# P times V of a sliding-window attention in 64x32 array tiles, with both row halves stored and added later

## The chip, the cores and the metric

The kernel runs on one core of a Trainium2 chip. A core has a matrix engine (TensorE, PE in the profile, with its weight loads as PEld), a vector engine (VectorE, DVE), a scalar engine (ScalarE, ACT), a general engine (GpSimd, POOL), a synchronisation engine that mostly issues transfers (SyncE, SP), and 16 DMA engines. The metric is the device time of one execution in microseconds (us); the median of the runs counts.

## The reference

A layer computes attention and an MLP on the same 2048 tokens of 512 features and mixes them with a gate per token:

```
q, k, v = split(x @ wqkv)            # 32 heads of 16
s = q @ k.T * 16**-0.5               # masked to 0 <= i - j < 256
a = softmax(s) @ v @ wo
b = gelu(layernorm(x) @ w1 + b1) @ w2 + b2     # 512 -> 1792 -> 512
out = g * a + (1 - g) * b            # g = sigmoid(sum(x * gate_w))
```

All of it is fp32. Each query sees itself and the 255 tokens before it, so a block of 128 keys meets at most three blocks of 128 queries.

## The kernel before

Products of q, k, v and of the MLP are made in a faster fp32 format in three terms (high x high, low x high, high x low). P times V alone is in plain fp32, and each of its matmuls leaves two records in the trace.

The kernel has three stages. The first (to about 148 us) makes q, k and v, stores q and k to DRAM in a stacked layout, and normalises the tokens. The second (148 to 486 us) is attention and the first MLP layer, woven together. The third (486 us on) is the second MLP layer (`mlp2`, 56 items of 12 matmuls) with the output projection (`attn_out`) at four places.

In the second stage the heads come in 8 groups p of four. Four kinds of work are ordered by a string of letters, the order table, which `run` walks through one letter at a time, and TensorE executes in that order:

- **S** (`s_pair`): scores of two heads for one block of queries. DVE reduces each to its row maxima (L377), which go through DRAM back into the stacked q.
- **T** (`st_pair`): transposed scores of two heads for one block kb of keys, maxima taken off within the matmul. ACT takes the exponential (L418) into a tile `p` (or `xq`) of 128 keys x 4 heads x 384 queries, POOL sets what is out of the window to 0 (L420).
- **P** (`pv`, L427): P times V. The four heads of a group stand in four column tiles of 32 of the array and run side by side. One P makes the output of two query blocks (256 queries) from up to four key blocks, in matmuls of 128 keys by 256 or 128 queries. V has a column of ones for each head, so the sum of the exponentials comes along. ACT copies the 256 columns to half of a tile (L443), and each second P sends the tile to `osc` in DRAM.
- **f** (`fill`): one step of an MLP unit of the first layer: two matmuls on the two row halves of the array (L639).

PSUM is a ring of four bank pairs, `b0` to `b3`. An MLP unit keeps one for its 24 steps; S, T and P take turns on the other three. Pools: `work` has six `p` tiles and nine `t` tiles in the second stage, `xq` gives two more P tiles (kb 3, 7, 11, 15). Work that is due later is put on a list (`after(k, ...)`) that advances by one with each key block in the second stage and with each item in the third. SP issues nearly all transfers, in its own program order.

In the third stage `attn_out(c)` starts for 512 queries at the items in `AO`. For each of four groups of heads it loads the attention output and the reciprocal sums from DRAM into tiles `or`, multiplies them on POOL (L822), splits the product into a high part on ACT and a low part on DVE, and multiplies by wo (L840). `attn_sums` makes the reciprocals from 16 small loads ahead of that. DVE makes the high and low parts of the hidden tiles (L706, L139) that `mlp2` multiplies, in the same queue.

The start of the kernel (`first_units`, L268) converts weights and the first tokens on ACT and takes low parts on DVE.

## Time and profile before

| | |
|---|---|
| median of 3 runs | 685.75 us (685.74 to 688.0) |
| profiled execution | 687.4 us, span 685.7 us |
| PE busy | 677.5 us (99%) |
| DVE, ACT, POOL busy | 473.4, 362.8, 277.6 us |
| granted TensorE clock, mean | 0.996 |
| moved by DMA | 137.95 MB |

The span runs from the first to the last instruction; the time of an execution has some more around it. A row of a group gives the line of the kernel, the engine, the operation, output and inputs, the shape, the count; behind the bar the busy time and the mean of one in ns; behind the second bar the idle time of the engine ahead of these instructions and what ended it. A row of a timeline gives the start in us, the length, the engine and line, and how many alike were merged. Shapes of matmuls read as weights, then moving data: `128*32 128x256` is 128 rows by 32 columns of weights and 256 columns streamed. Durations of matmuls include the way through the array, and neighbours overlap.

### The profile page before, as it was taken

The numbers are of one execution on the slowest core, as the hardware profiler recorded it, in microseconds if no ns is written. First come the engines' busy times: TensorE is split into PE (matmuls) and PEld (weight loads), VectorE is DVE, ScalarE is ACT, GpSimd is POOL, SyncE is SP. The second block draws the span as 40 slices with busy tenths as digits, with TensorE's granted clock in tenths as the row PEclk, the third lists the DMA queues.
The fourth block names the chain that finished last, engine by engine and source line by source line (L and its number), as shares of the span: only waits on it lengthen the run. The fifth ranks groups of instructions, "written<-read, shape, count | busy, mean of one in ns | idle before, by whom it ended". The sixth has DMA issues, their size and how long they took to land.

```text
span 685.7 us, 16341 instructions
## 1 busy us (share of the span) xinstructions
PE 677.5 (99%) x5738; PEld 543.2 (79%) x5738; DVE 473.4 (69%) x1495; ACT 362.8 (53%) x580; POOL 277.6 (40%) x553
## 2 busy tenths in 40 slices
PE   8999999999999999999999999999999999999997
PEld 6877777876778888788878778777788888888886
DVE  5378866698877877767877878786587453736623
ACT  6332223357776776777667668768763022324210
POOL 8210019816465655656547547647411030210300
PEclk9999999999999999999999999999999999999999
DMA  8899877876666677675676655736994371832801
GB/s 270 274 311 297 287 239 263 259 224 215 186 219 210 193 213 232 202 215 159 208 234 217 187 186 165 206 119 189 315 281 149 125 202 50 241 115 92 235 1 61
DMA packets 91446, 137.95 MB, mean 201 GB/s; under 512 B 15108, under 2 KB 38852, under 8 KB 91236
## 3 DMA queue, kind: packets, MB, share of 16 engines
q1 hardware_dynamic: 90324, 135.20, 63.2%
q8 instruction: 45, 0.74, 0.5%
q0 software_dynamic: 320, 1.05, 0.4%
q10 hardware_dynamic: 720, 0.66, 0.3%
q14 instruction: 37, 0.30, 0.1%
HBM read 81.53 MB, written 54.28 MB: 198 GB/s over the span
## 4 chain that ended last, share of the span: by engine, by line
PE 93%; DMA 4%; DVE 2%; ACT 1%; SPq 0%; issue 0%; DVEq 0%; ACTq 0%
PE ps_b L639 23%; PE ps_a L872 22%; PE ps_b L435 12%; PE ps_d L311 10%; PE ps_b L416 7%; PE ps_o L840 6%; PE ps_b L372 6%; PE ps_d L346 4%; DMA t<-in_xa 2%; PE ps_d L296 1%; DMA qk<-t 1%; DMA t<-in_wqk 1%; PE ps_x L372 1%; DVE us L879 0%; DVE xq L139 0%; ACT x L142 0%
## 5 line engine op out<-in xcount | busy, mean ns | idle before, releaser
L377 DVE CUSTOM_DVE_ANT_0 scr<-ps_b,wide 128x384 bf16<-128x384 f32 (+1 forms) x472 | 227.6, 530 | 63.6 <-PE ps_b L372 61.7
L639 PE MATMUL ps_b<-x,w 64*128 64x512 f32 x1344 | 208.6, 392 | 0.7 <-DVE t L139 0.7
L420 POOL TENSOR_SCALAR_AFFINE_SELECT p<-p 128x256 f32<-128x256 f32 x368 | 140.1, 411 | 129.2 <-ACT p L418 127.9
L418 ACT ACTIVATE p<-ps_b 128x768 f32<-128x768 f32 x192 | 146.6, 795 | 30.8 <-PE ps_b L416 23.3
L872 PE MATMUL ps_a<-x,h 128*128 128x512 f32 x648 | 149.0, 389 | 0.0
L872 PEld LDWEIGHTS ps_a<-x,h 128*128 128x128 f32 x648 | 121.6, 188 | 25.3
L639 PEld LDWEIGHTS ps_b<-x,w 64*128 64x128 f32 x1344 | 128.4, 186 | 10.2 <-DVE t L139 1.1
L416 PE MATMUL ps_b<-q,k 50*128 50x384 f32 (+5 forms) x512 | 89.9, 345 | 0.2 <-DVE mx L377 0.2
L372 PE MATMUL ps_b<-k,q 62*128 62x384 f32 (+3 forms) x472 | 81.9, 336 | 0.0
L822 POOL TENSOR_TENSOR or<-or,or 128x512 f32<-128x512 f32 x16 | 23.1, 1446 | 138.8 <-DMA or<-rd 133.5
L142 ACT ACTIVATE t<-ps_b 128x256 f32<-128x256 f32 (+1 forms) x116 | 52.8, 487 | 43.5 <-PE ps_b L435 35.2
L435 PE MATMUL ps_b<-p,v 128*32 128x256 f32 (+1 forms) x1472 | 71.8, 330 | 0.0
L416 PEld LDWEIGHTS ps_b<-q,k 50*128 50x128 f32 (+1 forms) x512 | 49.3, 184 | 16.7 <-DVE mx L377 3.6
L435 PEld LDWEIGHTS ps_b<-p,v 128*32 128x32 f32 x1472 | 42.4, 110 | 23.1 <-issue 2.9
L372 PEld LDWEIGHTS ps_b<-k,q 62*128 62x128 f32 (+1 forms) x472 | 46.5, 185 | 10.1 <-ACT p L418 1.4
L420 POOL TENSOR_SCALAR_AFFINE_SELECT xq<-xq 128x256 f32<-128x256 f32 x112 | 44.0, 418 | 22.1 <-ACT xq L418 21.1
L418 ACT ACTIVATE xq<-ps_b 128x768 f32<-128x768 f32 (+1 forms) x64 | 44.2, 706 | 14.1 <-PE ps_b L416 11.4
L142 ACT ACTIVATE t<-ps_d 128x512 fp32r<-128x512 f32 x32 | 19.0, 596 | 54.3 <-PE ps_d L311 49.3
L142 ACT ACTIVATE a<-or 128x512 fp32r<-128x512 f32 x16 | 10.1, 633 | 67.3 <-POOL or L822 67.3
L840 PE MATMUL ps_o<-wo,a 128*128 128x512 f32 x192 | 45.5, 389 | 0.0
L139 DVE TENSOR_TENSOR h<-e,h 128x512 fp32r<-128x512 f32 x54 | 39.6, 733 | 4.6
L377 DVE DVE_READ_ACCUMULATOR2_ANT mx<- 128x1 f32 x512 | 42.4, 83 | 0.0
(94 smaller groups left out, 744.9 us busy)
## 6 DMA issues: line engine op xcount, KB each, us to landing
qk<-t SPq DMA_DIRECT2D x72, 256.0 KB
hp<-t SPq DMA_DIRECT2D x54, 256.0 KB
e<-hp SPq DMA_DIRECT2D x54, 256.0 KB
k<-qk SPq DMA_DIRECT2D x112, 98.0 KB
q<-qk SPq DMA_DIRECT2D x112, 98.0 KB
osc<-t SPq DMA_DIRECT2D x30, 256.0 KB
w<-w SPq DMA_DIRECT2D x28, 256.0 KB
qk<-qk SPq DMA_DIRECT2D x24, 256.0 KB
```

What stands on the lines that cost most here:

```text
L139: eng.tensor_tensor(out=lo, in0=src, in1=f32(hi), op=ALU.subtract)
L142: act.activation(dst, src, AF.Copy)
L311: pe.matmul(o, a[:, dt * 128:(dt + 1) * 128], b[:, dt * C:(dt + 1) * C], start=n == 0, stop=n == 11)
L372: pe.matmul(o[:, e, :n], qs[pr][r:k, qb * 128:qb * 128 + 128], ks[pr][r:k, t0:t0 + n], start=True, stop=True)
L377: dve.tensor_tensor_reduce(out=sc[:, :n], in0=o[:, e, :n], in1=wide[:, 384 - n:], scale=1.0, scalar=NEG, op0=ALU.add, op1=ALU.max, accum_o ...
L416: pe.matmul(o[:, e, :w], ks[pr][r:k, kb * 128:kb * 128 + 128], qs[pr][r:k, kb * 128:kb * 128 + w], start=True, stop=True)
L418: act.activation(pt[:, :, :w], o[:, :, :w], AF.Exp, scale=0.25)
L420: pool.affine_select(out=pt[:, :, a:a + 128], in_=pt[:, :, a:a + 128], pattern=[[0, 2], [sgn, 128]], base=b, channel_multiplier=-sgn, comp ...
L435: pe.matmul(a[32 * h:32 * h + 32, at:at + w], vs[:, kb, v:v + 32], pts[p, kb][:, h, fr:fr + w], start=n == 0, stop=n == len(parts) - 1, sk ...
L639: pe.matmul(o[:, e], w[kt // 4][r:r + 64, k, m:m + 128], y[r:r + 64, a:a + C], start=n == 0, stop=n == 23)
L840: pe.matmul(a, hl[g][x][:, b * 128:b * 128 + 128], wos[g][:, k], start=n == 0, stop=n == 11)
L872: pe.matmul(accs[c][b], x[:, b * 128:(b + 1) * 128], w, start=f == 0 and n == 0, stop=f == FT - 1 and n == 2)
```

## The change

P times V takes four query blocks (512 queries) at once, in array tiles of 64 rows by 32 columns: two halves of the keys of a block times four heads, eight tiles. The upper 64 keys of each block accumulate in one bank of a pair, the lower 64 in the other. Since each half block has its own window of queries, the pieces are 320 columns wide at most, cut at the edges of the 512, and the order of the key blocks differs between the halves so that pieces of one width meet. ACT copies both banks at once into a tile `o` of 128 x 2 x 512, and one transfer stores both halves to `osc`, which has twice the size. The sums are added in `attn_sums`, and the outputs in `attn_out` on DVE, ahead of POOL's product. The reciprocals have a tag of their own in the `xq` pool, `t` has seven tiles for nine, the first output projection starts at item 9 (7 before), and the order table is a new one with 31 letters P for 63 (a last P stands behind it). At the start, the first tile of x is converted by DVE, as an addition of zeros.

```diff
-ORDER = ("TSTfffSfTSffffTSffTfTfSfTffSffTSffTfSfTfSffSPTSSTPSTTPSTffSfTfSffTffTSffTffSfSPTfSfTffTffTSfffSffSPT"
...
+ORDER = ("TfTffSffTfSfTSfffTSfTffTfSfTfSffTfSfTSffTSffSSPSTfffSffSffTfffSTffSffTfSffTfTffffSSPSTTSTSTSTTST"
+         "STffSffTSfffSffSPSffTfffTSfTffTffTTSffTfffSSPSfTfffTfSfTffSffTTffSfTffSfTfSfffTSffTffSPSTffffTfSfTff"
...
+         "SffTffSfSPSTSTTSTSTffSffTSfffTfTffffTTPfTTfffTffffTffffTTPffTfTfffTfTfffTffTfTffTfTfPfTfffTfTTfff")
...
-AO = (7, 16, 28, 42)
+AO = (9, 16, 28, 42)
...
-    osc = dram.tile([8, 128, S], F32, name="osc")
+    osc = dram.tile([2, 8, 128, S], F32, name="osc")
...
             for t in range(2):
                 if dt % 2 == 0:
                     k = slice(dt * 128, dt * 128 + 256)
                     copy(ws[t][:, 0, k], raws[t][:, k])
+                    if not dt and not t:
+                        hi(0, lambda h, x: dve.tensor_tensor(out=h, in0=x, in1=f32(blank), op=ALU.add))
                     lo_part(ws[t][:, 1, k], raws[t][:, k], ws[t][:, 0, k])
-                if t == 0:
-                    hi(dt)
+                if t == (not dt):
+                    if dt:
+                        hi(dt)
                     lo(dt)
...
-    def pv(p, j, last):
+    def pv(p, j):
         flush()
-        a = two()[:, 0]
-        parts = ((-1, 0, 128, 256), (-2, 0, 256, 128), (0, 0, 0, 256), (1, 128, 0, 128))[0 if j else 2:]
-        for n, (d, at, fr, w) in enumerate(parts):
-            kb = 2 * j + d
-            for h in range(4):
-                v = (4 * p + h) * VW
-                pe.matmul(a[32 * h:32 * h + 32, at:at + w], vs[:, kb, v:v + 32], pts[p, kb][:, h, fr:fr + w],
-                          start=n == 0, stop=n == len(parts) - 1, skip_group_check=True, tile_position=(0, 32 * h))
...
+        a = two()
+        ds = ((0, 1, 2, -1, 3, -2), (0, 1, -1, 2, -2, 3)) if j else ((0, 1, 2, 3),) * 2
+        for n in range(len(ds[0])):
+            for r in range(2):
+                d = ds[r][n]
+                kb = 4 * j + d
+                k = slice(64 * r, 64 * r + 64)
+                lo = max(0, 2 * d + r) if kb else 0
+                hi = min(8, 2 * d + r + 5)
+                for h in range(4):
+                    v = (4 * p + h) * VW
+                    pe.matmul(a[32 * h:32 * h + 32, r, lo * 64:hi * 64], vs[k, kb, v:v + 32],
+                              pts[p, kb][k, h, (lo - 2 * d) * 64:(hi - 2 * d) * 64],
+                              start=n == 0, stop=n == len(ds[0]) - 1, skip_group_check=True, tile_position=(64 * r, 32 * h))
+        s = get(("xq", "work")[j % 2], "o", 1, (128, 2, 512))
+        copy(s, a)
+        to = osc[:, p, :, j * C:(j + 1) * C].rearrange("r p q -> p r q")
+        if lt:
+            after(1, lambda: sp.dma_start(to, s))
         else:
...
+            pool.dma_start(to, s)
+        done.add(("o", p, j))
...
-    nt[0] = 9
+    for key, side in (("xq", "right"), ("work", "left")):
+        close_pool(key)
+        open_pool(key, side)
+    nt[0] = 7
...
-            dve.reciprocal(su, su)
-            sp.dma_start(view(rds[c], [128, 128], [1, 128]), su)
+            dve.tensor_tensor(out=su[:, 0], in0=su[:, 0], in1=su[:, 1], op=ALU.add)
+            dve.reciprocal(su[:, 0], su[:, 0])
+            sp.dma_start(view(rds[c], [128, 128], [1, 128]), su[:, 0])
...
-            for ts, d, step, off in ((os, osc, S, g * 256 * S + c * C), (rs, rds[c], 0, g * HG * C)):
+            for r, ts in enumerate((os, ot)):
                 ts.append(t2(tag="or"))
-                sp.dma_start(ts[g], view(d, [step, DH], [32 * S if step else C, HG], [1, C], off=off))
+                sp.dma_start(ts[g], view(osc, [S, DH], [32 * S, HG], [1, C], off=(r * 1024 + g * 256) * S + c * C))
+            rs.append(get("xq", "rd", 8, (128, C)))
+            sp.dma_start(rs[g], view(rds[c], [0, DH], [C, HG], [1, C], off=g * HG * C))
...
         def scale(g):
+            dve.tensor_tensor(out=os[g], in0=os[g], in1=ot[g], op=ALU.add)
             pool.tensor_tensor(out=os[g], in0=os[g], in1=rs[g], op=ALU.mult)
```

How this moves instructions shows at three places. In the rows, an L number is the line in the kernel they are from (the change's `pv` has its matmul at L444, T is L420 and S is L376 there), then output and inputs, then the columns written; `ps_b` is a bank pair of the ring, `k` and `q` are the stacks.

On TensorE before, the last P of the first group of heads and the first of the second:

```order
L639 MATMUL ps_b_489_2392<-x_260_1336,w_1541 128x512 x2
L435 MATMUL ps_b_505_2449<-p_2195,v_84 32x256 x4
L435 MATMUL ps_b_505_2449<-p_2155,v_84 32x128 x4
L435 MATMUL ps_b_505_2449<-p_2245,v_84 32x256 x4
L435 MATMUL ps_b_505_2449<-xq_2263,v_84 32x128 x4
L435 MATMUL ps_b_506_2467<-p_2353,v_84 32x256 x4
L435 MATMUL ps_b_506_2467<-p_2397,v_84 32x128 x4
L416 MATMUL ps_b_509_2485<-q_3_80,k_5_82 128x384 x2
```

The first takes four key blocks, the second two; each writes 256 columns of a bank pair of its own.

On TensorE now, the second P of the first group, with the two S ahead of it:

```order
L376 MATMUL ps_b_401_2001<-k_5_82,q_3_80 128x384 x2
L376 MATMUL ps_b_404_2008<-k_6_83,q_4_81 128x384 x2
L444 MATMUL ps_b_410_2021<-p_1719,v_84 32x320 x8
L444 MATMUL ps_b_410_2021<-p_1759,v_84 32x320 x8
L444 MATMUL ps_b_410_2021<-p_1887,v_84 32x256 x4
L444 MATMUL ps_b_410_2021<-p_1678,v_84 32x256 x4
L444 MATMUL ps_b_410_2021<-p_1678,v_84 32x192 x4
L444 MATMUL ps_b_410_2021<-p_1887,v_84 32x192 x4
L444 MATMUL ps_b_410_2021<-p_1929,v_84 32x128 x4
L444 MATMUL ps_b_410_2021<-p_1644,v_84 32x128 x4
L444 MATMUL ps_b_410_2021<-p_1644,v_84 32x64 x4
L444 MATMUL ps_b_410_2021<-p_1929,v_84 32x64 x4
```

Each step has four matmuls on the upper row half and four on the lower, of one width: 320, 320, 256, 192, 128 and 64. Six key blocks go in, where a P had four.

Right behind that P on TensorE now:

```order
L376 MATMUL ps_b_412_2072<-k_5_82,q_3_80 128x384 x2
L420 MATMUL ps_b_416_2085<-q_3_80,k_5_82 128x384 x2
L420 MATMUL ps_b_417_2091<-q_4_81,k_6_83 128x384 x2
L376 MATMUL ps_b_418_2097<-k_6_83,q_4_81 128x384 x2
L420 MATMUL ps_b_422_2109<-q_3_80,k_5_82 128x384 x2
L376 MATMUL ps_b_423_2115<-k_5_82,q_3_80 128x384 x2
L420 MATMUL ps_b_426_2122<-q_4_81,k_6_83 128x384 x2
L376 MATMUL ps_b_427_2128<-k_6_83,q_4_81 128x384 x2
L420 MATMUL ps_b_431_2141<-q_3_80,k_5_82 128x384 x2
L420 MATMUL ps_b_432_2147<-q_4_81,k_6_83 128x384 x2
```

These and four more S and T stand there with no step of the MLP between them; it is the longest such run of the new table.

More of the change, by code (lines that the diff above doesn't have):

```diff
@@ L181, in gated_mix_kernel @@
     open_pool("x", "right")
+    open_pool("xq", "right")
     open_pool("work")
@@ L187, in gated_mix_kernel, with x8 @@
     room += [get("work", "wv", DT - 1, (128, 2, 512), F32R) for _ in range(DT - 1)]
-    def x8(tag="x8", bufs=8, dt=F32R):
-        return get("x", tag, bufs, (128, 2048), dt)
+    def x8(key="x", bufs=8):
+        return get(key, "x8", bufs, (128, 2048), F32R)
     def wt():
@@ L245, in part, with hi @@
             return t[:, dt * C:(dt + 1) * C]
-        def hi(dt):
-            copy(part(h, dt), part(raw, dt))
+        def hi(dt, by=copy):
+            by(part(h, dt), part(raw, dt))
         def lo(dt):
@@ L425, in flush @@
             late.pop(0)()
-    def pv(p, j, last):
+    def pv(p, j):
         flush()
-        a = two()[:, 0]
-        parts = ((-1, 0, 128, 256), (-2, 0, 256, 128), (0, 0, 0, 256), (1, 128, 0, 128))[0 if j else 2:]
-        for n, (d, at, fr, w) in enumerate(parts):
-            kb = 2 * j + d
-            for h in range(4):
-                v = (4 * p + h) * VW
-                pe.matmul(a[32 * h:32 * h + 32, at:at + w], vs[:, kb, v:v + 32], pts[p, kb][:, h, fr:fr + w],
-                          start=n == 0, stop=n == len(parts) - 1, skip_group_check=True, tile_position=(0, 32 * h))
-        if j % 2 == 0:
-            acc[p] = t2()
-        s = acc[p]
-        o = j % 2 * 256
-        if last:
-            dve.tensor_copy(s[:, o:o + 256], a[:, :256])
-        else:
-            copy(s[:, o:o + 256], a[:, :256])
-        if j % 2:
-            to = osc[p, :, (j - 1) * 256:(j + 1) * 256]
-            if lt:
-                after(1, lambda: sp.dma_start(to, s))
-            else:
-                pool.dma_start(to, s)
-            done.add(("o", p, j))
+        a = two()
[17 more added lines that the diff above has]
+            after(1, lambda: sp.dma_start(to, s))
+        else:
+            pool.dma_start(to, s)
+        done.add(("o", p, j))
     def load_consts():
@@ L714, in attn_sums @@
     def attn_sums(c):
-        assert ("o", 7, 2 * c + 1) in done
-        su = small("su", 1, (128, 128))
-        for g in range(NG):
-            sp.dma_start(su[32 * g:32 * g + 32],
-                         view(osc, [32 * S, HG], [128, 4], [1, 128], off=(g * 256 + 16) * S + c * C))
+        assert ("o", 7, c) in done
+        su = small("su", 1, (128, 2, 128))
+        for r in range(2):
+            for g in range(NG):
+                sp.dma_start(su[32 * g:32 * g + 32, r],
+                             view(osc, [32 * S, HG], [128, 4], [1, 128], off=(r * 1024 + g * 256 + 16) * S + c * C))
         rds[c] = dram.tile([H, C], F32, name=nm("rd"))
         def inv():
-            dve.reciprocal(su, su)
-            sp.dma_start(view(rds[c], [128, 128], [1, 128]), su)
+            dve.tensor_tensor(out=su[:, 0], in0=su[:, 0], in1=su[:, 1], op=ALU.add)
+            dve.reciprocal(su[:, 0], su[:, 0])
+            sp.dma_start(view(rds[c], [128, 128], [1, 128]), su[:, 0])
         after(3, inv)
@@ L755, in gated_mix_kernel @@
     ls = [(p, qb, pr) for p in range(8) for qb in range(NB) for pr in range(2)][2 * (NB - LAG):]
-    lp = [(p, j) for p in range(8) for j in range(NB // 2)]
+    lp = [(p, j) for p in range(8) for j in range(NB // 4)]
     def run(order):
@@ L772, in run @@
                 if a:
-                    pv(*a, lt and not ls)
+                    pv(*a)
             else:
```

37 lines of the change are left out of this document (19 added, 18 removed).

## The prediction

> **What bounds the kernel now.** I read the page's busy shares first, then the chain that ended last, then the busy times by stage (columns: length, then PE, PEld, DVE, ACT and POOL busy, granted clock, DMA share, GB/s).
>
> ```profile
> PE 677.5 (99%) x5738; PEld 543.2 (79%) x5738; DVE 473.4 (69%) x1495; ACT 362.8 (53%) x580; POOL 277.6 (40%) x553
> PE 93%; DMA 4%; DVE 2%; ACT 1%; SPq 0%; issue 0%; DVEq 0%; ACTq 0%
> 148.00:486.00 338.00, 337.02 (x4250) 267.07 (x4250) 261.70 (x1058) 249.48 (x389) 198.54 (x493) 1.00 0.65 199
> 486.00:682.00 196.00, 195.81 (x864) 161.79 (x862) 109.27 (x176) 59.54 (x96) 24.87 (x20) 1.00 0.49 152
> ```
>
> TensorE sets the end: 99% busy, 93% of the chain, clock 1.00 in both late stages. The edit lies in the stage 148 to 486 us (attention and the first MLP layer); there DVE is 77% and ACT 74% busy, so only time taken off PE counts, as long as those two don't become late. A busy 99% hides something, though: the end of a matmul is modelled, so short pauses between matmuls don't show as idle. I therefore price PE work by start to start, not by busy time.
>
> ```profile
> 307.01 0.34 PE L372 MATMUL ps_b<-k,q 62*128 62x384 f32 x2
> 307.19 0.85 PE L639 MATMUL ps_b<-x,w 64*128 64x512 f32 x6
> 311.50 0.34 PE L372 MATMUL ps_b<-k,q 48*128 48x384 f32 x2
> 311.77 0.64 PE L435 MATMUL ps_b<-xq,v 128*32 128x256 f32 x8
> 312.22 1.05 PE L435 MATMUL ps_b<-p,v 128*32 128x128 f32 x24
> 313.20 0.62 PE L416 MATMUL ps_b<-q,k 64*128 64x384 f32 x4
> 300.80 0.64 PE L435 MATMUL ps_b<-xq,v 128*32 128x256 f32 x8
> 303.20 0.40 PE L435 MATMUL ps_b<-xq,v 128*32 128x128 f32 x8
> 303.53 0.62 PE L416 MATMUL ps_b<-q,k 64*128 64x384 f32 x4
> 346.38 4.04 PE ps_b L435 x96
> ```
>
> These are rows of PE's timeline and one of the chain. Each matmul of P times V leaves two records (two passes of fp32). A lone P, 32 records, takes 311.77 to 313.20 = 1.43 us; two in a row take 300.80 to 303.53 = 2.73 us; three (the chain's row, 96 records) 4.04 us. So one more P costs 1.30 us. Its four heads run side by side, and its pieces are 256+128+256+128 = 768 columns wide: 1.30/768 = 1.69 ns a column, both passes in. What is left, 1.43 - 1.30 = 0.13 us, is paid once on leaving a run of P's. Entering costs too: a score pair gives way to its successor after 0.18 us (307.01 to 307.19), but to a P after 0.27 us (311.50 to 311.77). A visit therefore costs 0.09 + 0.13 = 0.22 us beside its columns.
>
> **The change part by part.** *Columns streamed.* Before, each of 8 groups of heads has seven P's of 768 columns and a first one of 256 + 128 = 384: 8 x 5760 = 46,080. After, both row halves run at once if the array lets them, and a step lasts as long as its wider half. A later P has steps of 320, 320, 256, 192, 128 and 64 in both halves: 1280. The first of a group pairs 320/384, 320/320, 256/192 and 128/64: 1088. That is 8 x (3 x 1280 + 1088) = 39,424, or 6,656 fewer, times 1.69 ns = **-11.3 us**. Before and after in absolute terms: 78.0 and 66.7 us.
>
> *Visits.* The order table has 49 runs of P's before (63 letters and the one behind the table) and 32 after, none adjacent: 17 x 0.22 = **-3.7 us**.
>
> *Narrow passes.* The trace has no 64-wide pass of P times V. A weight load lasts 110 ns:
>
> ```profile
> L435 PEld LDWEIGHTS ps_b<-p,v x1472: 105/110/111, 159.4 to 484.9; 128*32 128x32 f32 x184
> L416 PEld LDWEIGHTS ps_b<-q,k 50*128 50x128 f32 (+1 forms) x512 | 49.3, 184 | 16.7 <-DVE mx L377 3.6
> ```
>
> A 64-wide pass streams in 64 x 1.69/2 = 54 ns. If a pass can't be shorter than the load, 24 visits x 2 passes x 56 ns = +2.7 us; if loads run ahead, 0. Loads seem to run ahead, since score pairs follow each other at 0.18 us with loads of 0.184, so I take **+0.7**, bounds 0 and 2.7. The Trainium skill ("TensorE: Matmul & The Clock Gate", section "LDWEIGHTS (loading the stationary operand)") says that a load takes its columns at 1.2 GHz, 27 ns for 32 columns. An estimate from that page: if the four heads' loads queue on one path, 107 ns a step, close to the 110 ns here, and the sum would come out 1.8 us later than mine. Nothing in this trace tells a queue of loads from a latency.
>
> *Copies out of PSUM.* 60 ACT copies of 256 columns and 4 DVE copies become 32 ACT copies of 1024.
>
> ```profile
> L142 ACT ACTIVATE t<-ps_b 128x256 f32<-128x256 f32 x60 | 22.9, 385 | 36.5 <-PE ps_b L435 35.2 <-ACT t L142 1.1
> L142 ACT ACTIVATE t<-ps_b 128x512 f32<-128x512 f32 x56 | 30.4, 596 | 6.9 <-PE ps_b L639 6.5
> L418 ACT ACTIVATE p<-ps_b 128x768 f32<-128x768 f32 x176 | 137.3, 813 | 28.7 <-PE ps_b L416 22.5 <-POOL xq L420 2.8 <-POOL p L420 0.8
> ```
>
> 256 columns more cost 211 to 217 ns, so a 1024-wide copy should take 1.03 us; 32 of them are 32.9 us against 60 x 0.385 = 23.1. ACT gets 9.8 us more in a stage where it idles 88. Queued behind a copy on ACT are the exponentials of the next T's, and the bank pair of a P stays taken 0.64 us longer, one of three that S, T and P share while an MLP unit holds the fourth. If all of the extra reached PE it would be 9.8 us, if none 0; I take **+1.5**, nearer nothing, since fills stand behind most P's.
>
> *Stretches without fills.* The order table is new. Its longest runs without a fill have 17 letters (S S P S T T S T S T S T T S T S T) and 11; before, there were 12 runs of 8 to 13, most with two or three P's as PE work in them.
>
> ```profile
> 303.67 0.39 ACT L142 ACTIVATE t<-ps_b 128x256 f32<-128x256 f32 x1 [0.92 <-PE ps_b L435]
> 304.02 1.51 ACT L418 ACTIVATE p<-ps_b 128x768 f32<-128x768 f32 x2
> 304.83 0.56 DVE L377 CUSTOM_DVE_ANT_0 scr<-ps_b,wide 128x384 bf16<-128x384 f32 x1 [1.44 <-PE ps_b L372]
> 305.80 0.08 DVE L377 DVE_READ_ACCUMULATOR2_ANT mx<- 128x1 f32 x1
> ```
>
> One exponential more takes 1.51 - 0.81 = 0.70 us, one S on DVE 304.83 to 305.80 = 0.97 us. Behind the P of the long run stand 8 T and 6 S: ACT 1.03 + 8 x 0.70 = 6.6 us, DVE 5.8 us, PE 14 x 0.18 = 2.5 us. With three bank pairs PE may lead ACT by two exponentials, so it waits about 6.6 - 1.4 - 2.5 = 2.7 us. The shorter run (5 T, 4 S behind its P) gives 1.03 + 3.5 - 1.4 - 1.6 = 1.5. Of 4.2 I take off 1.2 for the twelve that go: **+3.0**, bounds 0.5 and 6.
>
> *Start.* The first tile of x is converted on DVE now, so ACT does not have two conversions ahead of the first real matmul, which waited 0.4 us for ACT: **-0.3**.
>
> ```profile
> L296 PE MATMUL ps_d<-x,wx 128*128 128x512 f32 x24 | 6.1, 404 | 0.4 <-ACT x L142 0.4
> L819 SPq DMA_DIRECT2D or<-osc x16: 514/515/572, 501.7 to 640.2; - x16
> L822 POOL TENSOR_TENSOR or<-or,or x16: 1282/1304/1808, 509.5 to 648.4; 128x512 f32<-128x512 f32 x16
> L139 DVE TENSOR_TENSOR a<-or,a x16: 678/684/686, 518.6 to 652.9; 128x512 fp32r<-128x512 f32 x16
> ```
>
> *The added half at the output.* 16 DVE adds of 128x512 (0.68 us each by the last row, 10.9 in all) go into a stage where DVE is 109 of 196 us busy. They put something new at risk: the wait for a load from DRAM stood on POOL, where nobody else queued; now DVE waits first, and behind it stand the conversions of the MLP's hidden tiles that PE eats. In the trace the first product starts 509.5 - 501.7 = 7.8 us after its load was issued, and the add comes three items (of 12 matmuls: 32.64 us for 144 in the chain, 2.72 us an item) after the load, 8.2 us. That is near, but the first output projection now starts at item 9, not 7, behind the crowded part. **+0.4**, bounds 0 and 5.
>
> ```profile
> 624.69 32.64 PE ps_a L872 x144
> 486.00:496.00 10.00, 10.00 (x45) 8.26 (x44) 7.15 (x13) 5.46 (x10) 1.72 (x4) 1.00 1.02 362
> 506.00:516.00 10.00, 10.00 (x46) 8.28 (x45) 9.23 (x17) 4.92 (x9) 2.89 (x2) 1.00 0.87 227
> q1 hardware_dynamic: 90324, 135.20, 63.2%
> ```
>
> *Transfers.* The output of attention is stored twice as large: 32 x 256 KB more written (8.4 MB), 16 x 256 KB more read (4.2 MB). The main queue moved 135.2 MB in 63.2% of 685.7 us, 312 GB/s of its own time, so the stage of attention gets 27 us of DMA time on a share of 0.65, about 0.73. Hidden, unless transfers bunch: **0**. The two buffers that tag t loses (9 to 7) answer to the accumulators that P kept there and that have buffers of their own now.
>
> *Sum.* -11.3 - 3.7 + 0.7 + 1.5 + 3.0 - 0.3 + 0.4 = -9.7 us. The profiled execution had a span of 685.7 us and a time of 687.4; the median of the runs shown is 685.75, so the profiled one ran 1.65 us over it and the sum is taken off the median: **676 us**.
>
> **The rivals.** *All clean* (15%): new waits stay under other work, 685.75 - 15.3 = 670.5 us. For it: ACT and DVE idle a quarter of the stage. Against: the long run without fills.
>
> *The waits move to ACT* (18%): all of the copies' extra 9.8 and the upper 6 for the runs reach PE, with 0.7 for narrow passes: 685.75 - 15.3 + 16.5 = 687 us; with half of the copies' extra, 682; the case's middle is 684, about no change. For it: one engine copies two banks at once, and PE can't reuse them before. Against: 88 us of idle ACT. The Trainium skill ("TensorEngine Tiling (Array Packing)", section "Performance Considerations") warns of just this: tiling speeds up TensorE and not the copy out of PSUM, which should be spread over ScalarE and VectorE; here the copies leave DVE. By that rule this rival is the outcome; in the trace so far the copies are not what PE waits for (36.5 us of idle ACT stand before them, ended by PE).
>
> *Transfers or the add come late* (8%): the 27 us bunch in attention, or the add holds DVE at each of the first four loads, 5 us each with 2 items of lead: about 690 us. For it: a DMA share of 1.02 at 486 us. Against: 0.65 on average.
>
> *The two row halves do not run at once with four heads in each* (7%): then each half's columns count, 8 x (3 x 2560 + 1984) = 77,312, 130.9 us against 78.0, +52.9 - 3.7 + 5.3 gives 740 us. Break-even lies where 15% of the overlap is lost (9.7 of 64.2 us). Against it: the halves of an MLP unit (64-row tiles) do run in pairs, six of 512 columns in 0.85 us, and four heads run side by side now; only both together are not in the trace.
>
> **How the numbers follow.** 676 us has 52%, and the rivals 15, 18, 8 and 7. What a measurement can tell from no change is about 0.5%, 3.4 us. Faster than 682.3: 0.51 + 0.15 + 0.05 = 0.71. Within: 0.01 + 0.12 + 0.03 = 0.16. Slower: 0.01 + 0.05 + 0.07 = 0.13. The range, 667 to 689, takes in the clean case and the waits; the serial case and the worst of the transfers stay outside. The forecast's own range is 671 to 681.
>
> **What would show it.** A later P of 2.2 us start to start (1280 x 1.69), with the second half's records a few ns behind the first's; about 4.3 us if the halves take turns, and about 2.3 if narrow passes last as long as their load. ACT copies of 128x1024 at 1.03 us. PE idle or stretched before S and T behind the P of the long run, released by ACT. In the last stage, DVE's adds released by the load and no idle PE. The forecast is wrong if the stage 148 to 486 doesn't shrink by 7 to 14 us, or if the last stage grows from 196.

## The result

| | time | ratio to the kernel before |
|---|---|---|
| kernel before | 685.75 us | 1 |
| changed kernel | 696.6 us (693.0 to 698.7) | 1.0147, 95% interval 1.0099 to 1.0195 |

The change makes the kernel slower by 1.5%, where 676 us was forecast, with a range to 689. The profiled execution of the changed kernel took 696.15 us, with a span of 694.4. Its page begins, and its chain that ended last is shared out, like this:

```profile
PE 676.7 (97%) x6634; PEld 544.7 (78%) x6634; DVE 489.3 (70%) x1512; ACT 368.1 (53%) x551; POOL 275.3 (40%) x552
PE 69%; DMA 13%; DVE 7%; issue 3%; SPq 3%; ACT 2%; POOL 1%; DVEq 0%; ACTq 0%; POOLq 0%
```

TensorE's share of the chain fell from 93 to 69%; transfers rose from 4 to 13%, DVE from 2 to 7%. By stage (length, then PE, PEld, DVE, ACT, POOL busy, granted clock, DMA share, GB/s):

```profile
145.80:492.80 347.00, 335.55 (x5146) 268.97 (x5145) 259.57 (x1054) 253.83 (x359) 197.67 (x492) 0.99 0.73 215
493.00:691.00 198.00, 196.97 (x864) 161.65 (x863) 126.56 (x197) 60.73 (x97) 23.32 (x19) 1.00 0.60 179
```

From its first matmul to the first one of the last stage, the attention stage grew from 337.6 to 347.0 us, where it should have shrunk by 7 to 14; the last stage went from 196.1 to 197.9.

Where the time sits is seen better start to start, by the kind of work on TensorE. The table adds up, for each kernel named, all the time from the first matmul of a letter to the first matmul of the next letter of another kind (S, T, P, fill); a wait counts to the letter ahead of it. The experiments are told further on.

| attention stage, us | T | S | fills | P | sum |
|---|---|---|---|---|---|
| before | 49.6 | 45.7 | 157.6 | 84.7 | 337.6 |
| changed | 50.8 | 53.8 | 167.1 | 75.4 | 347.0 |
| new table, old tiles and stores | 48.7 | 52.2 | 163.0 | 83.7 | 347.7 |
| changed, half of the store | 50.2 | 53.4 | 163.0 | 72.1 | 338.8 |
| the same, banks freed | 43.7 | 48.2 | 163.4 | 75.0 | 330.3 |

So P times V did get shorter, by 9.3 us in the changed kernel and by 12.6 where half of the store is left out; S and the fills, which nobody touched, grew by 8.1 and 9.5.

A second table says what the delays were. For each letter that started more than 60 ns later after its forerunner than is usual for such a pair, it takes the delay and puts it down to what ended it, by the semaphore events in the trace; a delay within a stretch of half clock stands by itself. It is an inference from the trace: the sum of a row is surer than its split between ACT and DVE. Many of these delays are 0.1 to 0.5 us, and most don't show as idle time of TensorE.

| delays in us | ACT empties a bank | DVE empties a bank | a transfer | half clock |
|---|---|---|---|---|
| before | 3.0 | 3.8 | 0.5 | 0 |
| changed | 7.6 | 4.6 | 10.1 | 5.2 |
| new table, old tiles and stores | 3.8 | 4.7 | 2.1 | 5.7 |
| changed, half of the store | 8.8 | 5.0 | 2.5 | 3.7 |
| half of the store, fills spread | 9.4 | 7.9 | 1.6 | 0 |

Against before, the changed kernel has 9.6 us more of late transfers, 5.4 more of waits for a bank pair, and 5.2 at half clock.

The main queue moved more, and was taken longer (before: 135.20 MB, 63.2%):

```profile
q1 hardware_dynamic: 97380, 148.05, 70.0%
```

**The late transfers**, from the changed kernel's issues on SP, TensorE's rows around them, its chain, and the waits of TensorE and of SP's queue (in all, times, longest):

```profile
265.36 0.54 SPq L451 DMA_DIRECT2D osc<-o  x1
266.00 0.43 SPq L363 DMA_DIRECT2D k<-qk  x1
266.48 0.72 SPq L363 DMA_DIRECT2D q<-qk  x1
```

```profile
267.71 2.44 PE L444 MATMUL ps_b<-p,v 64*32 64x320 f32 x96
272.10 0.44 PE L376 MATMUL ps_b<-k,q 62*128 62x384 f32 x2 [1.95 <-DMA q<-qk]
```

```profile
266.48 5.48 DMA q<-qk
```

```profile
PE ps_b L376 <- DMA q<-qk: 5.7, 8, 1.9
...
SPq L400 <- DMA osc<-o: 14.7, 16, 1.8
```

The 512 KB store of a P goes out at 265.36, the load of stacked q that the next S needs a microsecond behind it; it lands 5.48 us after its issue, and TensorE stands idle for 1.95 us. SP itself waits 16 times for such a store to land before it goes on with its list, 14.7 us in all; before, there is one such wait, of 0.4 us. The semaphores in the trace tell why: 864 of SP's 875 transfers use the semaphore of the transfer eight places ahead and wait for that one to land. So the list has at most eight transfers on the way, and a store that lands late holds up what comes eight places behind it. SP's waits for landings add up to 13.5 us in the attention stage before, to 31.7 in the changed kernel and to 17.9 with half of the store.

The lead of a load of the stacks is counted here from the end of the issue of its last transfer (it has four) to the first S over its tokens. It is 7.05 us before (median of 56 loads, worked out from the rows of SP and TensorE; 5 of them under 4 us), and 4.08 in the changed kernel (26 under 4).

**The long run without fills and the half clock**, on TensorE, on ACT, and by stretches:

```profile
168.81 2.45 PE L444 MATMUL ps_b<-p,v 64*32 64x320 f32 x96
171.19 0.44 PE L376 MATMUL ps_b<-k,q 62*128 62x384 f32 x2
...
177.20 1.13 PE L644 MATMUL ps_b<-x,w 64*128 64x512 f32 x4
```

```profile
171.34 1.02 ACT L141 ACTIVATE o<-ps_b 128x1024 f32<-128x1024 f32 x1 [1.67 <-PE ps_b L444]
172.26 6.00 ACT L422 ACTIVATE p<-ps_b 128x768 f32<-128x768 f32 x8
```

```profile
172.00:178.00 6.00, 5.25 (x26) 3.27 (x28) 5.67 (x24) 5.93 (x9) 4.77 (x14) 0.72 0.94 288
178.00:182.00 4.00, 4.00 (x26) 3.35 (x24) 2.77 (x13) 1.06 (x2) 1.85 (x6) 0.56 0.46 131
```

The 14 letters behind the P take 171.19 to 177.20, 6.0 us where 14 x 0.18 = 2.5 would do, while ACT runs eight exponentials without a gap. That much had been seen coming (2.7 us). What had not is that the clock falls to half at 174.7 us and stays there until 181.5, 6.8 us, 4.3 us of it behind the run, over fills and scores. The pause at 272.10 is followed by another stretch at half clock, of 3.4 us. Before, attention has none at all.

### The profile page after: what moved, and what is told of

Same layout as the page of the kernel before. It is cut to its first block, busy times and chain, and to the rows that moved or that the text cites. A ratio compares the mean times of both kernels' runs of the same rounds, so it can differ in the third digit from the quotient of the medians.

```text
span 694.4 us, 18172 instructions
## 1 busy us (share of the span) xinstructions
PE 676.7 (97%) x6634; PEld 544.7 (78%) x6634; DVE 489.3 (70%) x1512; ACT 368.1 (53%) x551; POOL 275.3 (40%) x552
## 4 chain that ended last, share of the span: by engine, by line
PE 69%; DMA 13%; DVE 7%; issue 3%; SPq 3%; ACT 2%; POOL 1%; DVEq 0%; ACTq 0%; POOLq 0%
PE ps_a L884 18%; PE ps_b L644 18%; PE ps_b L444 8%; PE ps_o L852 6%; PE ps_b L376 6%; PE ps_b L420 5%; DMA q<-qk 5%; PE ps_d L315 4%; PE ps_d L350 2%; DMA or<-osc 2%; DMA qk<-t 2%; DMA t<-in_xa 2%; DVE scr L381 2%; DVE x L138 2%; ACT p L422 1%
## 5 line engine op out<-in xcount | busy, mean ns | idle before, releaser
L424 POOL TENSOR_SCALAR_AFFINE_SELECT p<-p 128x256 f32<-128x256 f32 x480 | 183.1, 414 | 151.0 <-ACT p L422 148.8
L422 ACT ACTIVATE p<-ps_b 128x768 f32<-128x768 f32 (+2 forms) x256 | 188.0, 775 | 39.0 <-PE ps_b L420 33.5
L376 PE MATMUL ps_b<-k,q 62*128 62x384 f32 (+2 forms) x472 | 86.2, 354 | 7.6 <-DMA q<-qk 5.7
L420 PE MATMUL ps_b<-q,k 64*128 64x384 f32 (+5 forms) x512 | 91.4, 345 | 1.8 <-DVE mx L381 0.6
L444 PE MATMUL ps_b<-p,v 64*32 64x320 f32 (+4 forms) x2816 | 74.1, 349 | 0.6 <-DVE mx L381 0.3
L444 PEld LDWEIGHTS ps_b<-p,v 64*32 64x32 f32 x2816 | 55.1, 106 | 22.7 <-issue 5.0
L376 PEld LDWEIGHTS ps_b<-k,q 62*128 62x128 f32 (+1 forms) x472 | 47.3, 187 | 25.9 <-issue 5.4
L420 PEld LDWEIGHTS ps_b<-q,k 64*128 64x128 f32 (+1 forms) x512 | 51.2, 188 | 19.7 <-DVE mx L381 5.3
L141 ACT ACTIVATE a<-or 128x512 fp32r<-128x512 f32 x16 | 10.1, 633 | 76.5 <-POOL or L834 76.5
L315 PE MATMUL ps_d<-x,w 128*128 128x512 f32 x192 | 46.4, 392 | 0.0
L350 PE MATMUL ps_d<-wv,x 128*128 128x512 f32 x192 | 46.1, 392 | 0.0
L852 PEld LDWEIGHTS ps_o<-wo,a 128*128 128x128 f32 x192 | 36.0, 188 | 8.9 <-ACT a L141 1.0
```

Source lines behind the costliest of these rows:

```text
L141: act.activation(dst, src, AF.Copy)
L315: pe.matmul(o, a[:, dt * 128:(dt + 1) * 128], b[:, dt * C:(dt + 1) * C], start=n == 0, stop=n == 11)
L376: pe.matmul(o[:, e, :n], qs[pr][r:k, qb * 128:qb * 128 + 128], ks[pr][r:k, t0:t0 + n], start=True, stop=True)
L420: pe.matmul(o[:, e, :w], ks[pr][r:k, kb * 128:kb * 128 + 128], qs[pr][r:k, kb * 128:kb * 128 + w], start=True, stop=True)
L422: act.activation(pt[:, :, :w], o[:, :, :w], AF.Exp, scale=0.25)
L424: pool.affine_select(out=pt[:, :, a:a + 128], in_=pt[:, :, a:a + 128], pattern=[[0, 2], [sgn, 128]], base=b, channel_multiplier=-sgn, comp ...
```

## The experiments

Each was timed beside the kernel before on its chip. The first kernels say what each piece of the change costs.

**Half of the store.** The third stage reads the upper half twice, so that the sums over the lower 64 keys of each block are left out; all work on the engines stays.

```diff
-            after(1, lambda: sp.dma_start(to, s))
+            after(1, lambda: sp.dma_start(to, s[:, 0]))
```

> The changed kernel, but only the upper half of the keys is stored (256 KB a transfer, not 512) and the third stage reads that half twice, so the output leaves out the lower half; tiles, order table and number of transfers stay. The changed kernel lost 18 us of PE time in attention to pauses of over 0.25 us, most of them before an S that waits for a load of stacked q and k, and two half-clock windows (6.8 and 3.4 us). Theory A (the doubled stores stand ahead of the stack loads on the DMA engines): most of these waits go, about 685 us (683 to 689). Theory B (the new order table puts each S too soon behind its load, whatever else is moved): the same within 2 us, 694 to 698 us.

Measured: 687.4 us, ratio 1.0005 (0.9986 to 1.0024). The doubled store costs 9 us, and the delays by transfers fall from 10.1 to 2.5 us. But 11 us of the forecast are still missing.

**The store a key block later, and the loads of the stacks ahead of the transfers on the list.**

```diff
-            after(1, lambda: sp.dma_start(to, s))
+            after(2, lambda: sp.dma_start(to, s))
```

```diff
     def block(p, kb):
-        tick()
         if kb % 2 == 0:
             ...load_stacks...
+        tick()
```

> The changed kernel with the store of a P issued one key block later, which is a block without stack loads; bytes, tiles and order table stay. Theory A (a 512 KB store issued right ahead of four stack loads delays them): the waits shrink, 686 to 692 us. Theory B (short lead in the order table): no change within 2 us of 696.6.

> The changed kernel with the stack loads issued ahead of all other transfers due at the same key block (stores of P, stores of MLP halves, copies of q and k, maxima). Each load starts some 1.5 to 3 us earlier and has nothing of its block ahead of it. Both theories expect a gain, A because the store is behind the loads, B because the lead grows by 2 us on 4.1 (median): 685 to 691 us. If the time does not move, the loads are not what PE waits for.

Measured: 695.05 (1.0113, 1.0072 to 1.0153) and 699.7 (1.0156, 1.0092 to 1.0219): neither helps. With the loads first, their lead grows to 7.42 us, and the wait goes to the next transfer in the queue, the maxima that T needs:

```profile
PE ps_b L420 <- DMA q<-md: 5.5, 4, 2.9
...
PE ps_b L376 <- DMA q<-qk: 1.0, 2, 0.6
```

So the place of one transfer in the list is not it: in either order something that TensorE needs comes late behind the 512 KB.

**The new order table with the old tiles.** Two old P's in the place of each new one, the old store, the old last stage.

```diff
             elif a == "P":
                 a = lp.pop(0)
                 if a:
                     pv(*a, lt and not ls)
+                    pv(*lp.pop(0), lt and not ls)
```

> The kernel before with the new order table, each letter P doing two of the old P's (128x32 tiles, 256 columns each, one 256 KB store): the new table without the new tiles, the new stores, the new buffers and the adds. The columns of P cost the 11.3 us that the new tiles save, the visits do not. Theory B (the table's short lead makes the waits): slow, 700 to 706 us. Theory A (the stores make them): about the kernel before, 682 to 690 us.

Measured: 694.4 us, ratio 1.0109 (1.0070 to 1.0148): the table by itself costs 7.5 us, its fewer visits to P included. That lies between the two theories. Its stage has 5.7 us at half clock (6.8 us long at 176.5, 3.4 at 466.6, each behind one of the two runs without fills), 1.6 more of late transfers and 1.7 more of bank waits than before.

**Doubled bytes in the kernel before.** Each store of P times V is made twice, to two places; the copy is never read.

```diff
-                after(1, lambda: sp.dma_start(to, s))
+                after(1, lambda: [sp.dma_start(t, s) for t in (to, osd[...])])
```

> The kernel before with each store of P times V made twice, to two places in DRAM, as two transfers of 256 KB one behind the other; the copy is never read. So the bytes of the change in the order and the tiles of before. Theory 1 with lead (doubled bytes hurt the changed kernel because its loads of stacked q and k stand only 4.1 us ahead of their first reader in the middle, against 7.1 before): before hides most of it, 686-689. Rival (the bytes themselves cost it, wherever they stand): as in the changed kernel against its half store, +9: 693-697.

Measured: 689.8 us, ratio 1.0059 (1.0039 to 1.0079), 4 us, between the two theories. The median lead of the loads falls from 7.05 to 5.69 us. The bytes alone take 4 us with the old order and 9 in the changed kernel. There is less lead to take there (5.38 us with the half store), which would explain the difference; no run changed the lead alone, and 512 KB in two transfers was not tried in the changed kernel.

**The fills spread over the two long runs**, alone, with the half store, and with the halves added in SBUF ahead of one 256 KB store.

```diff
-... "SSPSTTSTSTSTTSTSTffSffTSfffSffSPS" ...
+... "SfSfSPfSfTfSSfTfSTfSfTfSTfTfSTfSfPSf" ...
```

```diff
+        def add():
+            dve.tensor_tensor(out=s[:, 0], in0=s[:, 0], in1=s[:, 1], op=ALU.add)
+
         if lt:
-            after(1, lambda: sp.dma_start(to, s))
+            after(1, add)
+            after(2, lambda: sp.dma_start(to, s[:, 0]))
```

> The changed kernel with one change: in its order table the two long runs without a fill step (17 letters in the first group of heads, 11 in the last) are broken up, by spreading the fill steps that stand around them evenly over about 70 and 40 places; the order of S, T and P, and every transfer, stay. Theory 1 (the changed kernel lost about 8 us to the two runs and the half-clock windows that followed them at 174.7 and 458 to 466, and about 9 to late loads behind doubled stores, two costs that add): the pauses at 172 to 178 and 463 to 467 and the half-clock windows behind them go, attention falls from 347 to 340-343, the time to 688-692. Theory 2 (the pauses only move, since the ring of banks and the vector engine's maxima set them, not the runs): the time stays at 694-698. Theory 3 (all of the loss comes from late transfers): no change, 696.

> The same spread order, and only the upper half of each result is stored (256 KB in the place of 512) and read in the place of both, so that the sums of the lower 64 keys of each block are left out of the output; all instructions on the engines stay. Theory 1 (two separate costs): both go, attention 329-333 us, the time 677-682, close to what was forecast for the change. Theory 2 (the pauses only move): as with the half store alone, 686-689. Theory 3 (late transfers are all of it): 686-689 too, since the half store alone has those out.

> The tiles and the spread order as before, but the two halves are added in SBUF: ACT copies both banks as in the change, a key block later DVE adds the lower half to the upper (32 instructions of 512 columns, some 0.6-0.7 us each by its other subtractions of that size), and another key block later one transfer of 256 KB stores the sum, with the third stage as it was in the kernel before. The computation is whole. Theory 1: as the half store with the spread order, and 32 x 0.65 = 21 us more on DVE, which is busy 260 of 347 us in attention, so 0-4 us of it come through: 677-685, faster than the kernel before. Theory 2 and 3: 686-691. If DVE's queue is what S and T wait for, the adds stand ahead of maxima: 688 or more.

Measured: 697.65 (1.0190, 1.0165 to 1.0215), 687.8 (1.0033, 1.0016 to 1.0050) and 692.7 (1.0093, 1.0074 to 1.0112). Theory 1 fell. The attention stage of the spread alone, and then of the spread with the half store, a row of each trace:

```profile
147.00:494.00 347.00, 335.98 (x5146) 263.34 (x5144) 259.29 (x1053) 253.58 (x358) 198.60 (x492) 1.00 0.72 215
```

```profile
147.50:487.50 340.00, 332.85 (x5145) 261.30 (x5145) 261.02 (x1056) 253.67 (x359) 198.35 (x492) 1.00 0.63 197
```

The lengths are 347.0 and 340.0 us, as without the spread (347.0 and 338.8), though the clock is whole or nearly so. With the half store, spreading took the half clock away (3.7 us of delays), and the waits for a bank pair grew from 13.8 to 17.3 us in its place. So it is not two places: with the fills spread, the waits for the three bank pairs came up elsewhere. The add in SBUF saves the bytes and pays on DVE: maxima of S stand behind it, and DVE's share of the bank waits goes from 7.9 to 13.2 us.

**The bank pairs freed.** The exponentials of T and the maxima of S read a constant in SBUF in the place of the pair that TensorE has written, so that it may be written again at once. The attention that comes out then means nothing.

```diff
-            dve.tensor_tensor_reduce(out=sc[:, :n], in0=o[:, e, :n], in1=wide[:, 384 - n:], ...
+            dve.tensor_tensor_reduce(out=sc[:, :n], in0=wide[:, 128:129].broadcast_to((128, n)), ...
...
-        act.activation(pt[:, :, :w], o[:, :, :w], AF.Exp, scale=0.25)
+        act.activation(pt[:, :, :w], wide[:, 128:130].unsqueeze(2).broadcast_to((128, 2, w)), ...
```

> The changed kernel with the half store (256 KB, the lower half left out), and the exponentials of T and the maxima of S read a constant in SBUF in the place of the bank pair that TensorE has just written, so that the attention that comes out means nothing. ACT and DVE do the same number of instructions of the same size, but no bank pair has to wait for them: TensorE may write it again as soon as it likes. Theory 1 (some 20 us of small waits, 0.1 to 0.5 us each, are S, T and fills that wait until ACT or DVE has emptied one of the three bank pairs; the kernel before has about 8 of them; the order table brought them): attention falls from 338.8 us to 320-325, the time to 668-674. Theory 2 (the waits sit elsewhere: P behind the masks on POOL, S behind its loads, switches of the array): attention 331-339, the time 679-687.

> The same freeing of the bank pairs in the kernel before: exponentials and maxima read a constant, everything else stays, so that the attention that comes out means nothing. Theory 1: its bank waits are some 4-6 us only, attention 332-334, the time 680-682; the difference to the run with the half store is then the tiles' own gain, forecast at 14. Theory 2: no change, 685-686.

> The changed kernel whole, with its 512 KB stores, and the bank pairs freed in the same way (exponentials and maxima read a constant; the attention that comes out means nothing). Tells whether late loads and bank waits add: theory 1, the late loads stay and cost what they cost with the banks in use (8 us), 676-682; if the two overlap, so that TensorE loses the same time once, 684 or more, or as little as 670-674 if the loads were late only because the banks held the order back.

> The new order table with the old column tiles (two old P in the place of each new one, old stores), and the bank pairs freed as above, so that the attention that comes out means nothing. With the banks in use this took 694.4, 8 above the kernel before. Theory 1 (the table costs by bank waits and the half-clock windows behind them): attention falls from 347.7 to 331-335, the time to 679-683, as the kernel before with free banks. Theory 2 (the table costs otherwise): it stays at 690 or more.

Measured: 702.6, 698.9, 702.1 and 702.6 us, all four 13 us or more over the kernel before. These runs don't answer the question, since the edit changed a load: with both operands in SBUF the maxima took longer, and POOL's masks beside them. The rows of DVE and POOL, first of the changed kernel, then of the run with the half store:

```profile
L381 DVE CUSTOM_DVE_ANT_0 scr<-ps_b,wide 128x384 bf16<-128x384 f32 (+1 forms) x472 | 228.3, 530 | 70.3 <-PE ps_b L376 68.4
L424 POOL TENSOR_SCALAR_AFFINE_SELECT p<-p 128x256 f32<-128x256 f32 x480 | 183.1, 414 | 151.0 <-ACT p L422 148.8
```

```profile
L381 DVE CUSTOM_DVE_ANT_0 scr<-wide 128x384 bf16<-128x384 bf16 (+1 forms) x472 | 302.2, 705 | 0.0
L424 POOL TENSOR_SCALAR_AFFINE_SELECT p<-p 128x256 f32<-128x256 f32 x391 | 240.4, 655 | 31.8 <-ACT p L422 27.5 <-PE ps_b L644 4.2
```

DVE had become the limit, 302 us of maxima and another 36 of reading the accumulators. So the maxima were cut to three quarters of their columns, and one run freed T's pairs alone.

```diff
+            k = n * 3 // 4
-            ... in0=wide[:, 128:129].broadcast_to((128, n)), in1=wide[:, 384 - n:], ...
+            ... in0=wide[:, 128:129].broadcast_to((128, k)), in1=wide[:, 384 - k:], ...
```

> The changed kernel with the half store, and only the exponentials of T read a constant in SBUF (the attention that comes out means nothing); the maxima of S read their bank pair as in the kernel. In the run before this one with both freed, the maxima took 706 ns from SBUF where they take 530 from PSUM, so that DVE itself became late; the exponentials kept their 795 ns. So only the waits for ACT's release go, some 9 of 22 us by the trace of the half store, and with them perhaps the half-clock windows (3.4 us). Theory 1 (bank waits): attention falls from 338.8 to 328-333, the time to 676-682. Theory 2 (the waits sit elsewhere): 336-340, 685-689.

> The changed kernel with the half store, exponentials and maxima read a constant in SBUF, and the maxima only over three quarters of their columns (the attention that comes out means nothing), so that one takes about 530 ns (706 x 3/4), as from PSUM in the kernel. So the engines' loads are those of the kernel and no bank pair of S or T waits for them. Theory 1: attention 320-326, the time 668-675. Theory 2: 333-340, 682-689.

> The kernel before with the same freeing: exponentials and maxima read a constant, maxima over three quarters of the columns (the attention that comes out means nothing). Theory 1: its bank waits are few, attention 331-335, the time 679-683. Theory 2: 685-686.

> The new order table with the old column tiles and old stores (694.4 with the banks in use), with the same freeing: exponentials and maxima read a constant, maxima over three quarters of the columns (the attention that comes out means nothing). Theory 1 (the table costs by bank waits): the time falls to 680-684, as the kernel before with free banks. Theory 2 (the table costs otherwise, as by late loads or by its stretches without fills): 688-694.

| | banks in use | both freed |
|---|---|---|
| before | 685.75 | 689.3 (1.0055, 1.0029 to 1.0081) |
| new table, old tiles | 694.4 | 686.2 (0.9998, 0.9984 to 1.0013) |
| new table, new tiles, half store | 687.4 | 678.1 (0.9897, 0.9868 to 0.9925) |
| the same, T's pairs alone freed | | 689.7 (1.0056, 1.0035 to 1.0078) |

The three kernels with both freed begin the stage with a pause of 2.6 to 3.8 us and a stretch of half clock, which the kernels with the banks in use don't have (the trace puts the pause down to a conversion on DVE). From the second group of heads on, the stage takes, one row from each kernel's trace, in before, the half store, before freed and the half store freed, and then in the new table with the old tiles, in use and freed:

```profile
187.50:485.70 298.20, 298.17 (x3803) 238.50 (x3801) 227.67 (x918) 219.43 (x342) 175.67 (x433) 1.00 0.64 198
```

```profile
189.20:485.50 296.30, 293.18 (x4630) 237.37 (x4626) 224.64 (x909) 224.54 (x319) 176.37 (x435) 0.99 0.65 197
```

```profile
189.70:487.20 297.50, 297.38 (x3802) 240.81 (x3800) 241.22 (x903) 211.12 (x343) 227.54 (x435) 1.00 0.63 195
```

```profile
188.10:475.90 287.80, 286.11 (x4630) 240.46 (x4626) 238.10 (x902) 219.31 (x319) 228.09 (x436) 1.00 0.66 203
```

```profile
190.30:494.80 304.50, 301.57 (x3814) 236.31 (x3810) 227.20 (x915) 218.98 (x342) 177.55 (x435) 0.99 0.62 192
```

```profile
188.00:482.70 294.70, 294.59 (x3814) 243.90 (x3810) 237.38 (x905) 210.39 (x342) 227.40 (x438) 1.00 0.65 199
```

Freeing the banks is worth 0.7 us to the kernel before, 8.5 to the new order with its own tiles and 9.8 to the new order with the old ones; DVE and POOL are even busier there than in the real kernels and ACT nearly as busy, so it is not their load that was taken away. With the banks freed the new order is 9.7 us shorter than the old one with the new tiles and 2.8 with the old tiles, in seven of eight groups; 7/8 of the 3.7 us forecast for the visits are 3.2. So the table costs nothing where the banks are free. That bears out theory 1 in its kind: the new order pays 8 to 10 us to bank pairs that are not yet emptied, of which some 1.7 us are a stretch of half clock of 3.4 us, which both its kernels have here with the banks in use and neither has with them freed. The sizes did not come as expected: 678.1 and 686.2 us lie between what the two theories said, 689.3 above both. In attention 8.5 us went for the 13 to 19 expected, in part since a maximum still took 584 ns there, not 530. With T's pairs alone freed nothing was gained: ACT's part of the waits fell from 8.8 to 1.9 us and DVE's rose from 5.0 to 11.2. So the pairs look short of both engines' time together: where ACT no longer ends a wait, DVE does.

**The exit of P shared**, the first bank by ACT, the second by DVE, with the half store and with the whole one.

```diff
-        copy(s, a)
+        copy(s[:, 0], a[:, 0])
+        dve.tensor_copy(s[:, 1], a[:, 1])
```

> The changed kernel with the half store (lower half left out), and the exit of each P shared: ACT copies the first bank (some 0.6 us), DVE the second, in the place of one ACT copy of 1.03 us over both. Theory 1a (ACT is what is late: it ended 8.8 us of the waits behind bank pairs here, against 3.8 with the old tiles, and the long copy stands ahead of the exponentials): the pair comes free 0.4 us sooner 32 times and ACT has 13 us less to do, 687.4 becomes 681-685. Theory 1b (the ring is short of both engines' time, as the run with T's pairs alone freed says, where the waits went over to DVE): what ACT gains DVE loses, 32 copies of some 0.4-0.5 us ahead of maxima, 686-691.

> The same shared exit in the changed kernel whole, with its 512 KB stores. Theory 1a: 696.6 becomes 690-694; theory 1b: 695-700. In both the doubled stores stay, so it should stand 7-11 above the run with the half store.

Measured: 705.5 us both (1.0267, 1.0220 to 1.0315; 1.0280, 1.0242 to 1.0318), worse than either theory, and the whole store no longer makes a difference. DVE's row with the half store tells why:

```profile
L449 DVE COPY o<-ps_b 128x512 f32<-128x512 f32 x30 | 20.7, 690 | 32.4 <-ACT o L141 30.3 <-DMA hp<-t 1.6 <-DMA k<-qk 0.5
```

Both copies write one tile, so DVE's waited for ACT's, a microsecond each time with the maxima queued behind, and took 690 ns more. The edit lengthened the exit it should have shortened, and how much ACT's long copy alone costs stays open. What it does show is that 53 us more on DVE, waited or worked (32.4 + 20.7), went with 18 us more for the kernel.

Of the versions here that compute everything, the kernel before is the fastest.

## Why the prediction was wrong, step by step

- **Columns and visits (-11.3 and -3.7): right in their sum.** The eight tiles run at once. A later P takes 168.81 to 171.19 = 2.38 us to the next letter. The first of a group:

```profile
342.82 1.93 PE L444 MATMUL ps_b<-p,v 64*32 64x320 f32 x64 [0.15 <-DVE mx L381]
344.68 0.44 PE L376 MATMUL ps_b<-k,q 62*128 62x384 f32 x2
```

  That is 1.86 us. 24 x 2.38 + 8 x 1.86 = 72.0 us; the forecast's parts that fall in these rows make 66.7 + 32 x 0.13 + 0.7 = 71.6.
- **Narrow passes (+0.7, bounds 0 and 2.7): too small, within the bounds.** By the forecast's columns alone a later P would take 1280 x 1.69 + 130 = 2.29 us and a first one 1088 x 1.69 + 130 = 1.97. The later ones take 0.09 more, 24 x 0.09 = 2.2 us. The first ones take 0.11 less, 0.9 us in all, and all eight take 1.86. That is the time of the longer half's own 1024 columns (1024 x 1.69 + 130 = 1.86). So the forecast's "a step lasts as long as its wider half" does not hold there: the halves don't wait for each other step by step. The two errors leave +1.3, so that 71.6 comes so near 72.0 partly by luck.
- **Copies out of PSUM (+1.5, bounds 0 and 9.8): too small.** The copy itself is as forecast:

```profile
L141 ACT ACTIVATE o<-ps_b 128x1024 f32<-128x1024 f32 x32 | 32.8, 1026 | 47.3 <-PE ps_b L444 30.3
```

  But with it in the place of the short ones, the bank waits that ACT ends go from 3.8 us (new table, old tiles) to 8.8 (half store). The two differ in the P's as well as in their exits, so the copy's own part is only argued. "Nearer nothing, since fills stand behind most P's" was the choice that failed: 22 of the 32 P's are followed by an S and 9 by a fill.
- **Stretches without fills (+3.0, bounds 0.5 and 6): the waits there came, but the rest of the table and the half clock were missed.** 3.5 us at the long run (2.7 forecast), and 2.0 at the short one (1.5 forecast; its 9 letters take 462.31 to 465.92 = 3.6 us, where 9 x 0.18 = 1.6 would do). The half clock was not in the sum at all, and the waits in all other places were put at nothing. The table by itself costs 7.5 us (4.8 to 10.2). It was priced by its two worst places; with the fills spread over these the time stayed, since the waits came up elsewhere. The old table has nine runs of 8 to 13 letters without a fill, not the twelve that the forecast took off.
- **Transfers ("hidden, unless transfers bunch": 0): wrong, and the largest miss, 9 us.** The mean share was forecast well (0.73, and 0.73 it is); what went with the 9 us was single loads that landed late behind 512 KB, and SP's list that waited for the stores to land. The rows from which the risk could be read were at hand: only 7 us from the issue of a load to its S, against 0.8 us per 256 KB at 312 GB/s for each store put ahead.
- **Start (-0.3): did not come.** The first matmul with a converted weight starts at 6.03 us (6.06 before), but the group of 24 is through later: the next one starts at 12.63 us (12.18 before). The weight that ACT converts is late there.
- **The added half (+0.4): fits, and is not told apart.** The last stage takes 196.3 to 196.4 us in most of the kernels that have the adds, against 196.1 before; but two kernels with a new table and without the adds take 196.3 and 196.4 too. The 197.9 of the profiled execution has another 1.5, and its chain goes through two loads that took 8 us each, ahead of the third projection:

```profile
598.07 7.79 DMA or<-osc
605.92 8.14 DMA or<-osc
```

The forecast's sum was -9.7, the outcome +10.1 (by the ratio) to +10.9 (by the medians). By the runs: the table alone +7.5; the tiles on top of it -7.0, where P times V became 11.6 us shorter (83.7 to 72.1) and 5 us more of bank waits that ACT ends came in; the doubled store +9. By the two tables, the kernel with half of the store has 12.7 us more of delays than before (20.0 against 7.3) and 12.6 less of P times V. So two steps failed. The waits that the new order brings were priced at 4.5 us (+1.5 and +3.0) and took the whole gain; the doubled store was priced at nothing and took 9 us more. The rivals "the waits move to ACT" and "transfers come late" both came true, each in part, and the forecast had treated them as alternatives of 18 and 8% rather than as costs that add.

## What to carry to other kernels

When a change shortens work on the bound engine, look at the two things that had been hidden under it before pricing the gain: how long each small load is issued ahead of its reader, in us, against what the change puts in front of it in the same queue; and how long each PSUM bank is held, by all engines together. Here a mean DMA share of 0.73 and engines idle a quarter of the time said nothing on either. Most delays of 0.1 to 0.5 us did not show as idle time of TensorE: add up starts to starts by kind of work, and test with a kernel that frees the banks while every engine does about the same work.

## What the runs showed of the hardware

- **Half clock after short waits.** TensorE was granted half clock for 6.8 us from 174.7, within the run at 171 to 177. Its longest single delay until then was 0.6 us (ahead of 172.41, where 0.42 us show as idle), and its work in the run would have taken 2.5 of the 6.0 us. Each stretch of half clock inside the attention stage lasts 3.4 or 6.8 us; one of 3.4 follows a single pause of 2 us (272.10). The Trainium skill ("TensorE: Matmul & The Clock Gate", section "A second HAM failure mode: psum-queue depth-cycling") says that a TensorE which idles for short whiles between groups, as it cycles through PSUM, loses and regains its clock; the trace agrees. The forecast had not used it. At the long run it was worth some 2 us, an estimate from the trace: from 177.2 to 181.5 TensorE did 4.3 us of fills and scores at half speed.
- **DVE and POOL slow each other down when the maxima have both operands in SBUF.** A maximum takes 530 ns on the mean with one operand in PSUM and 705 with both in SBUF; POOL's masks go from 414 to 655 ns beside it, with nothing about them changed. That it is the two engines together, and not SBUF as such, shows within the first run with both freed, of 702.6 us (medians, worked out from the starts and lengths in its trace). There a maximum over 384 columns takes 549 ns where POOL does nothing meanwhile and 744 where POOL works; in the changed kernel, with the operand in PSUM, it takes 553 either way. The Trainium skill ("GPSIMD Engine Reference", section "8. Key points") says that GpSimd shares its SBUF interfaces with VectorE and is in contention with DVE instructions that have two SBUF inputs; the rows agree. So an experiment that moves an operand of DVE into SBUF can change two engines' speed.
- **Eight 64x32 tiles in plain fp32 do run side by side**, four heads in each of two row halves: their records start 6 to 8 ns apart, and the next pass of 320 columns follows 0.27 us behind (169.11 to 169.38), which is 320 x 1.69/2. So the halves don't take turns.
